# The MLP takes one chunk at a time, scores and maxima keep four PSUM banks, and 1.5 conversions of weights a slot in the first batch, not 1.2

## The chip, the cores and the metric

The kernel runs on one core of a Trainium2 chip. The metric is the device time of one execution in microseconds. It was 1240.38 us before the change, the median of three runs (1237.52 to 1241.49).

## What is computed

Attention with a decay, for 8 batches of 8 heads with 576 positions of size 64, and behind it an MLP with a squared ReLU on all 4608 tokens of width 512, with 2048 hidden units.

```python
scores = scale * np.matmul(q, k.transpose(0, 1, 3, 2))
cum = np.cumsum(np.log(np.clip(f, 0.0001, 1.0)), axis=-1)
decay = cum[:, :, :, None] - cum[:, :, None, :]
scores = np.where(causal, -1000000000.0, scores + decay)
scores = scores - np.max(scores, axis=-1, keepdims=True)
attn = np.exp(scores)
attn = attn / (np.sum(attn, axis=-1, keepdims=True) + 1e-09)
x = (attn @ v), heads side by side          # 4608 x 512
h = np.maximum(x @ w_in, 0.0)
out = h * h @ w_out
```

The two weight matrices come as 64-bit words, two 32-bit halves each.

## The kernel before

**Slots.** The program is written out by one loop over slots `n`. A slot is one unit of scores of one head; a head has six, a batch 48, and there are 384. In slot n the kernel writes the score matmul and the exponential of that unit (`score`; L363 and L365 on TensorE for heads below 14, L369 and L372 from head 14 on; L382 on ScalarE) and the product with the values of the unit two slots back (L430, or L407 to L409). From head 14 on the probabilities are split into two parts first (L397 on ScalarE, L398 on VectorE). The row maxima of a head are found ahead of its scores in six units of their own: a matmul (L324) into a PSUM bank and a reduction by VectorE out of it (L330), which frees the bank. Loads, the division (`finish`) and the preparation of heads (`prep`) stand at fixed slots in the tables at the end of the kernel. Each engine and SP's DMA queue execute in the order in which the loop writes; nothing overtakes on an engine.

**Weights.** 32 weight tiles of 512 KB (`w_in` and `w_out` in turn) have to be turned from 64-bit words into two parts of 32 bits. `weight_ops` is a generator of that work: two steps to begin with, then five a tile, four with an operation of VectorE (L189, L194, L199, L201) and the last with a cast by ScalarE (L206) and four subtractions by GpSimd (L210). Its loads (L169 on SP's queue) run up to four tiles ahead. `RATES` says how many steps a slot takes: its fifth number holds from slot 0 to slot 52, the sixth from slot 53 until the work is done.

**MLP.** The tokens are cut into 18 chunks of 256. A step `(c, fc)` of chunk c works on 128 of the hidden units: `mlp1` (twelve matmuls, L501, into bank 4; then L509 to L512 on ScalarE and VectorE) and, a step later, `mlp2` (six matmuls, L524, which add up in the two banks `o0` and `o1` over all 16 steps). A half step is one of the two. `mlp1` of step fc needs weight tile 2 fc, `mlp2` tile 2 fc + 1, and a step is begun when both are converted. Each time, `fill` writes as many half steps as a straight line from 0 to 64 over slots 53 to 104 asks for (two chunks in that time; once the weights are done, the line is drawn anew from where it stands); if `next_step` finds none that can be done, it leaves the rest to later slots. Before the change `next_step` takes chunk 0's next step if its weights are there, and otherwise chunk 1's, which walks over the same weights behind it.

**Banks.** PSUM has eight banks, given out in turn by use.

```python
    banks = {"av": [0, 6], "s": [1, 2, 3], "m": [4, 5, 7], "h": [4], "o0": [6], "o1": [7]}
```

Here `s` are the scores, `m` the maxima, `av` the products with the values, `h` the result of `mlp1`. From the first step of the MLP on `m` is empty, and maxima then take their bank from `s`. While chunks 0 and 1 are both under way, four banks hold sums, and `s` has two.

Of the kernel before, what the change touches and what calls it, by code (L numbers as in the profile page):

```python
# [36 lines left out]
def decay_attention_relu2_kernel(  # L37
# [26 lines left out]
    NF = w_in.shape[0]  # L64
# [18 lines left out]
    banks = {"av": [0, 6], "s": [1, 2, 3], "m": [4, 5, 7], "h": [4], "o0": [6], "o1": [7]}  # L83
# [75 lines left out]
    split_w = []  # L159
# [315 lines left out]
    mst = {}  # L475

    def split_x(c, finished):

        if c >= NCHUNK:
            return  # L480
        if ("x", c) not in mst:
            mst["x", c] = [wk.tile([P, NCC, T], F32R, name=x, bufs=1) for x in xnames[c % 2]], c * T
        (xh, xl), t0 = mst["x", c]
        while t0 < (c + 1) * T and t0 // S < finished:
            b = t0 // S
            t1 = min((b + 1) * S, (c + 1) * T)
            o, i = slice(t0 - c * T, t1 - c * T), slice(t0 - b * S, t1 - b * S)
            nc.vector.tensor_copy(out=xh[:, :, o], in_=xts[b][:, :, i])
            nc.vector.tensor_tensor(
                out=xl[:, :, o], in0=xts[b][:, :, i], in1=xh[:, :, o].bitcast(F32), op=ALU.subtract,  # L490
            )
            t0 = t1
        mst["x", c] = (xh, xl), t0

    def mlp1(c, fc):
        xh, xl = mst["x", c][0]
        ph = bank("h")
        w = split_w[2 * fc].rearrange("p s (c f) -> p s c f", f=P)
        for k, (s, x) in enumerate(((1, xh), (0, xh), (0, xl))):
            for cc in range(NCC):  # L500
                nc.tensor.matmul(  # L501
                    ph[:, :T], w[:, s, cc], x[:, cc, :],
                    start=(cc == 0 and k == 0), stop=(cc == NCC - 1 and k == 2),
                )
        r = wk.tile([P, T], F32, name="r", bufs=1)
        g = wk.tile([P, T], F32, name="g", bufs=1)
        gh = wk.tile([P, T], F32R, name="gh")
        gl = wk.tile([P, T], F32R, name="gl")
        nc.scalar.activation(out=r, in_=ph[:, :T], func=AF.Relu)  # L509
        nc.vector.tensor_tensor(out=g, in0=r, in1=r, op=ALU.mult)  # L510
        nc.scalar.activation(out=gh, in_=r, func=AF.Square)  # L511
        nc.vector.tensor_tensor(out=gl, in0=g, in1=gh.bitcast(F32), op=ALU.subtract)  # L512
        mst["g", c, fc] = (gh, gl)

    def mlp2(c, fc):
        if fc == 0:
            mst["o", c] = [bank(f"o{t}") for t in range(NTT)]
        gh, gl = mst.pop(("g", c, fc))
        w = split_w[2 * fc + 1]
        for t in range(NTT):  # L520
            po = mst["o", c][t]
            ts = slice(t * P, (t + 1) * P)
            for k, (g, s) in enumerate(((gh, 1), (gl, 0), (gh, 0))):
                nc.tensor.matmul(  # L524
                    po, g[:, ts], w[:, s],
                    start=(fc == 0 and k == 0), stop=(fc == NF - 1 and k == 2),
                )
            if fc == NF - 1:
                osb = wk.tile([P, DM], F32, name="osb")
                nc.scalar.copy(out=osb, in_=po)  # L530
                nc.sync.dma_start(out=out[c * T + t * P:c * T + (t + 1) * P, :], in_=osb)

    ahead = [0] * NCHUNK
# [3 lines left out]
    def next_step():  # L537

        for c in range(NCHUNK):
            fc = ahead[c]  # L540
            if fc < NF and len(split_w) >= 2 * (fc + 1):
                return c, fc
            if fc < NF and c > 0:
                return None

    def mlp_half(finished):
        if halves[0] % 2:
            if len(steps) > 1:
                mlp2(*steps[-2])
        else:  # L550
            step = next_step()
            if step is None:
                return False
            c, fc = step
            if fc == 0:
                if c == 0:
                    banks.update(s=[1, 2, 3, 5], m=[], av=[0])
                if c == 1:
                    banks.update(s=[1, 2], o0=[3], o1=[5])
                if c == 2:  # L560
                    banks.update(s=[1, 2, 3, 5], o0=[6], o1=[7])
                split_x(c, finished)
            if fc > 0 and ("x", c + 1) not in mst and (c != 1 or ahead[0] == NF):
                split_x(c + 1, finished)
            mlp1(c, fc)
            ahead[c] += 1
            steps.append(step)
        halves[0] += 1
        return True
# [2 lines left out]

    RATES = (1, 0, 2, 0, 1.2, 2.8)
    LAG = 2
    NA = H * NU

# [29 lines left out]
    def fill(n, part):  # L608

        b = sum(r <= n for r in ready)  # L610
        if b == 0:
            return
        r0 = ready[b - 1]
        r1 = ready[b] if b < B else r0 + H * NU
        limit, before = (2 * NF * (x * S // T) for x in (b, b - 1))
        goal = before + (limit - before) * (n - r0 + part) / (r1 - r0)
        if b == 1 and len(split_w) == NW:

            if not pace:
                pace.append((n + part, halves[0]))  # L620
            n0, h0 = pace[0]
            goal = h0 + (limit - h0) * (n + part - n0) / (r1 - n0)
        while halves[0] < min(goal, limit):
            split_last()
            if not mlp_half(b):
                break
# [4 lines left out]
    def cv(k):  # L631
        owed[0] += k
        convert(int(owed[0]))
        owed[0] -= int(owed[0])
# [53 lines left out]
    for n in range(-2 * NU, last_slot + 1):  # L688
# [17 lines left out]
        for do in events.get((n, 0), ()):  # L706
            do()
        wr = RATES[0 if n < -9 else 1 if n < -6 else 2 if n < -3 else 3 if n < 0 else 4 if n < ready[0] else 5]
        cv(wr / 2)
# [6 lines left out]
    while halves[0] < 2 * NCHUNK * NF:  # L716
        mlp_half(B)
# [42 lines left out]
```

## Time and profile before

| | |
|---|---|
| median of 3 runs | 1240.38 us |
| the profiled execution | 1240.59 us, of which the span is 1238.9 us |
| TensorE matmuls | 1186.2 us, 96% of the span |
| VectorE / ScalarE / GpSimd | 63% / 57% / 33% |
| first matmul of the MLP (L501) | at 110.95 us |
| chunk 0 done, chunk 1 done (first L530 of each) | at 223.3 and 278.6 us |

The span is what the profiler sees of the program, from its first instruction to its last. PE is TensorE, PEld its loading of weights, DVE VectorE, ACT ScalarE, POOL GpSimd, SP the engine whose queue issues most transfers (SPq). In a time line a row has the start, the duration, the engine, line and operation, what is written and read, and in brackets how long the engine stood idle before it and what ended that. In a table by stretches a row has the stretch, its length, the busy time and the number of instructions of each engine, then the granted clock of TensorE (PEclk, 1.00 is full), the busy share of the transfer engines and what they moved in GB/s. A group of instructions has its busy time, the mean duration of one in ns, and the idle time before them.

### The profile page before, as it was taken

What the parts mean: (1) busy time and instruction counts of PE and PEld (TensorE: products, weight loads), DVE (VectorE), ACT (ScalarE), POOL (GpSimd) and SP (SyncE); (2) the same over time, 40 slices, a digit from 0 to 9 for tenths busy, and PEclk for the clock granted to TensorE, in tenths of its full rate; (3) what the DMA queues carried; (4) which work ended last, traced back from release to release, by engine and by line L of the source; (5) the groups of instructions that cost most, each with busy time, mean ns of one, the idle gap of its engine ahead of it and who ended that gap; (6) DMA issues with size and microseconds to landing.
All of it is one profiled execution on the core that took longest, in us unless ns stands there. A gap on an engine that the chain in (4) does not pass through costs nothing.

```text
span 1238.9 us, 23313 instructions
## 1 busy us (share of the span) xinstructions
PE 1186.2 (96%) x7652; PEld 1051.3 (85%) x7652; DVE 778.6 (63%) x2044; ACT 701.6 (57%) x1720; POOL 411.1 (33%) x670
## 2 busy tenths in 40 slices
PE   5877998899999999999999999999999999999998
PEld 3655887778999899999999989998999899999997
DVE  6748876657676767666656666677676767533332
ACT  3644565456666666665565656666666666632332
POOL 3544446333333333333223233334333333200000
PEclk9998998899999999999999999999999999999999
DMA  7766540212121112121202121211121212000000
GB/s 201 173 161 169 147 122 16 52 32 58 41 58 36 49 35 54 41 58 27 58 17 53 31 58 36 54 36 49 42 58 41 58 41 57 13 27 1 18 18 18
DMA packets 114977, 71.62 MB, mean 58 GB/s; under 512 B 96908, under 2 KB 96908, under 8 KB 114856
## 3 DMA queue, kind: packets, MB, share of 16 engines
q1 hardware_dynamic: 113736, 66.00, 21.4%
q0 software_dynamic: 1120, 4.13, 1.5%
q8 instruction: 61, 1.00, 0.3%
q14 instruction: 60, 0.49, 0.1%
HBM read 59.90 MB, written 9.87 MB: 56 GB/s over the span
## 4 chain that ended last, share of the span: by engine, by line
PE 54%; ACT 1%; issue 1%; POOL 1%; DVE 0%; DMA 0%; SPq 0%; POOLq 0%; DVEq 0%
PE bank L501 22%; PE bank L524 21%; PE bank L407 2%; PE bank L372 2%; PE bank L409 2%; PE bank L324 2%; PE bank L408 2%; PE bank L369 2%; DMA den<-rdr 0%; ACT ph L397 0%; ACT den L446 0%; ACT r L509 0%; ACT p L382 0%; POOL p L384 0%; POOL v L310 0%
## 5 line engine op out<-in xcount | busy, mean ns | idle before, releaser
L524 PE MATMUL bank<-w,gh 128*128 128x512 f32 x1152 | 415.7, 401 | 0.0
L501 PE MATMUL bank<-xh,w 128*128 128x256 f32 x2304 | 332.2, 287 | 1.8 <-DVE tcol L330 1.7
L501 PEld LDWEIGHTS bank<-xh,w 128*128 128x128 f32 x2304 | 303.7, 191 | 9.9 <-DVE tcol L330 1.9
L398 DVE TENSOR_TENSOR pl<-p,ph 128x320 fp32r<-128x320 f32 (+4 forms) x300 | 186.5, 622 | 199.2 <-ACT ph L397 188.4
L524 PEld LDWEIGHTS bank<-w,gh 128*128 128x128 f32 x1152 | 218.6, 190 | 38.4
L524 PE MATMUL bank<-w,gl 128*128 128x512 f32 x576 | 227.5, 395 | 0.1
L509 ACT ACTIVATE r<-bank 128x256 f32<-128x256 f32 x288 | 110.5, 384 | 204.2 <-PE bank L501 192.1
L384 POOL TENSOR_SCALAR_AFFINE_SELECT p<-p 128x128 f32<-128x128 f32 (+1 forms) x250 | 82.1, 329 | 419.5 <-ACT p L382 275.2
L510 DVE TENSOR_TENSOR g<-r 128x256 f32<-128x256 f32 x288 | 126.0, 437 | 143.0 <-ACT r L509 142.4
L397 ACT CAST ph<-p 128x320 fp32r<-128x320 f32 (+4 forms) x300 | 124.4, 415 | 151.7 <-POOL p L384 150.0
L501 PE MATMUL bank<-xl,w 128*128 128x256 f32 x1152 | 185.8, 284 | 0.0
L501 PEld LDWEIGHTS bank<-xl,w 128*128 128x128 f32 x1152 | 159.7, 192 | 0.0
L330 DVE CUSTOM_DVE_ANT_0 bank<-bank,mz 128x256 f32<-128x256 f32 (+4 forms) x320 | 133.3, 433 | 40.9 <-PE bank L324 31.6
L382 ACT ACTIVATE p<-bank 128x320 f32<-128x320 f32 (+4 forms) x300 | 116.1, 387 | 65.1 <-PE bank L372 52.9
L512 DVE TENSOR_TENSOR gl<-g,gh 128x256 fp32r<-128x256 f32 x288 | 127.3, 442 | 35.8 <-ACT p L382 1.4
L324 PE MATMUL bank<-rk 66*128 66x320 f32 (+9 forms) x384 | 112.0, 323 | 32.2 <-DVE tcol L330 15.4
L511 ACT ACTIVATE gh<-r 128x256 fp32r<-128x256 f32 x288 | 120.5, 418 | 9.1
L524 PEld LDWEIGHTS bank<-w,gl 128*128 128x128 f32 x576 | 109.8, 191 | 14.3 <-DVE gl L512 0.9
L324 PEld LDWEIGHTS bank<-rk 66*128 66x128 f32 (+3 forms) x384 | 69.5, 188 | 44.8 <-DVE tcol L330 19.3
L210 POOL TENSOR_TENSOR w<-osb,w 128x128 fp32r<-128x128 f32 x128 | 72.3, 593 | 94.7 <-ACT w L206 64.6
L407 PE MATMUL bank<-pl,vh 128*65 128x320 f32 (+4 forms) x350 | 97.0, 277 | 2.3 <-ACT den L446 2.3
L408 PE MATMUL bank<-ph,v 128*64 128x320 f32 (+4 forms) x350 | 94.8, 271 | 0.0
(82 smaller groups left out, 1557.9 us busy)
## 6 DMA issues: line engine op xcount, KB each, us to landing
qkraw<-in_qk SPq DMA_DIRECT2D x50, 288.0 KB
v<-in_v SPq DMA_DIRECT2D x62, 160.0 KB
out<-osb SPq DMA_DIRECT2D x36, 256.0 KB
den<-rdr SPq DMA_DIRECT2D x62, 144.0 KB
w<-in_w_in SPq DMA_DIRECT2D x16, 512.0 KB
w<-in_w_out SPq DMA_DIRECT2D x16, 512.0 KB
rk<-in_qk POOLq DMA_DIRECT2D x14, 288.0 KB, 4.4
rl<-in_qk SPq DMA_DIRECT2D x14, 288.0 KB
```

What stands on the lines that cost most here:

```text
L324: nc.tensor.matmul(ps[:m, :n], st["r2"][:rows, q0:q0 + m], st["kl0"][:rows, k0:k0 + n], start=True, stop=True,)
L330: nc.vector.tensor_tensor_reduce(out=ps[:m, :n], in0=ps[:m, :n], in1=mz[:m, mo:mo + n], op0=ALU.add, op1=ALU.min, scale=-1.0, scalar=init, ...
L382: nc.scalar.activation(out=p[:kn, :n], in_=ps[:kn, :n], func=AF.Exp, scale=SCALE)
L397: nc.scalar.copy(out=ph[:, :n], in_=p[:, :n])
L398: nc.vector.tensor_tensor(out=pl[:, :n], in0=p[:, :n], in1=ph[:, :n].bitcast(F32), op=ALU.subtract,)
L407: nc.tensor.matmul(acc[:D + 1, o], vh, pl[:, i], start=first, stop=False)
L408: nc.tensor.matmul(acc[:D, o], vl, ph[:, i], start=False, stop=False)
L501: nc.tensor.matmul(ph[:, :T], w[:, s, cc], x[:, cc, :], start=(cc == 0 and k == 0), stop=(cc == NCC - 1 and k == 2),)
L510: nc.vector.tensor_tensor(out=g, in0=r, in1=r, op=ALU.mult)
L511: nc.scalar.activation(out=gh, in_=r, func=AF.Square)
L512: nc.vector.tensor_tensor(out=gl, in0=g, in1=gh.bitcast(F32), op=ALU.subtract)
L524: nc.tensor.matmul(po, g[:, ts], w[:, s], start=(fc == 0 and k == 0), stop=(fc == NF - 1 and k == 2),)
```

## The change

`next_step` takes the chunks strictly in order: if the weights of the next step of the earliest unfinished chunk are not there, nothing is done. So two chunks are never under way together; the sums are always in banks 6 and 7, and `s` keeps its four banks from slot 53 to the end. The condition that held back `split_x` of chunk 2 goes with it. The fifth rate is 1.5 in place of 1.2.

```diff
         for c in range(NCHUNK):
             fc = ahead[c]
-            if fc < NF and len(split_w) >= 2 * (fc + 1):
-                return c, fc
-            if fc < NF and c > 0:
-                return None
+            if fc < NF:
+                return (c, fc) if len(split_w) >= 2 * (fc + 1) else None
...
                     banks.update(s=[1, 2, 3, 5], m=[], av=[0])
-                if c == 1:
-                    banks.update(s=[1, 2], o0=[3], o1=[5])
-                if c == 2:
-                    banks.update(s=[1, 2, 3, 5], o0=[6], o1=[7])
                 split_x(c, finished)
-            if fc > 0 and ("x", c + 1) not in mst and (c != 1 or ahead[0] == NF):
+            if fc > 0 and ("x", c + 1) not in mst:
                 split_x(c + 1, finished)
...
-    RATES = (1, 0, 2, 0, 1.2, 2.8)
+    RATES = (1, 0, 2, 0, 1.5, 2.8)
```

What it does to the order is shown at three places. First TensorE at slots 91 and 92, where the first two units of head 16's maxima stand (L324), with a score (L369, L372) and a product with the values (L407 to L409) between them. Before:

```order
L324 MATMUL bank2_2582<-rk_0_68 128x256
L369 MATMUL bank1_2585<-rk_1_69 128x192
L372 MATMUL bank1_2585<-rl_2276 128x192
L407 MATMUL bank0_2591<-pl_2530,vh_1_73 65x320
L408 MATMUL bank0_2591<-ph_2529,v_2467 64x320
L409 MATMUL bank0_2591<-ph_2529,vh_1_73 65x320
L324 MATMUL bank2_2595<-rk_0_68 128x320
```

After, where the first unit, in bank2, stands in front of an `mlp2` of six matmuls, of which the last is shown:

```order
L524 MATMUL bank7_2213<-w13_918,gh_2479 128x512
L369 MATMUL bank3_2564<-rk_1_69 128x192
L372 MATMUL bank3_2564<-rl_2265 128x192
L407 MATMUL bank0_2570<-pl_2498,vh_1_73 65x320
L408 MATMUL bank0_2570<-ph_2497,v_2436 64x320
L409 MATMUL bank0_2570<-ph_2497,vh_1_73 65x320
L324 MATMUL bank5_2574<-rk_0_68 128x320
```

Before, both units use bank2; now the second has bank5, and the score between them bank3.

Second, TensorE from slot 78 to the first of head 14's maxima in slot 79. Before, from the end of the `mlp2` in slot 77 on:

```order
L524 MATMUL bank5_1915<-w3_357,gh_1951 128x512
L363 MATMUL bank2_2028<-rl_71 128x320
L430 MATMUL bank0_1903<-ph_1966,v_1677 128x320
L501 MATMUL bank4_2049<-xh0_1067,w26_1957 128x256 x8
L501 MATMUL bank4_2049<-xl0_1068,w26_1957 128x256 x4
L363 MATMUL bank1_2070<-rl_71 128x320
L365 LDWEIGHTS mz_66
L365 MATMUL bank1_2070<-p_67,mz_66 128x128
L430 MATMUL bank0_2075<-pl_2007,v_1677 128x256
L430 MATMUL bank0_2075<-ph_1966,v_1677 128x128
```

There an `mlp2` (six matmuls from weight tile 5) follows, and then the maximum. After, from the end of slot 77 on:

```order
L430 MATMUL bank0_1947<-pl_1967,v_1728 66x64
L363 MATMUL bank5_2040<-rl_71 128x320
L430 MATMUL bank0_1947<-ph_2006,v_1728 128x320
L363 MATMUL bank1_2063<-rl_71 128x320
L365 LDWEIGHTS mz_66
L365 MATMUL bank1_2063<-p_67,mz_66 128x128
L430 MATMUL bank0_2068<-pl_2026,v_1728 128x256
L430 MATMUL bank0_2068<-ph_2006,v_1728 128x128
L501 MATMUL bank4_2073<-xh0_1113,w30_2031 128x256 x8
L501 MATMUL bank4_2073<-xl0_1114,w30_2031 128x256 x4
L324 MATMUL bank2_2097<-rk_0_68 128x256
```

Slots 77 and 78 now have no half step of the MLP, and in slot 79 the `mlp1` of chunk 0's last step, which reads weight tile 30, stands in front of the maximum.

Third, SP's queue around the values of heads 5 and 6 in the first batch (`v`, and for head 6 `w31`, whose buffer it borrows; `cmp`, `rdr` and `den` belong to the division, `w11` and so on are weight tiles). Before:

```order
L460 DMA cmp_613<-den_490 64x1x9 x2
L169 DMA w11_618<-in_w_out 128x1024
L277 DMA v_627<-in_v 128x5x64
L465 DMA rdr_675<-cmp_613 128x9
L260 DMA rl_70<-in_qk 64x1152
L247 DMA rl_70<-cum_dr_74 2x576
L169 DMA w12_695<-in_w_in 128x1024
L352 DMA rl_70<-tcol_643 1x128x1 x4
L352 DMA rl_70<-tcol_643 1x64x1
L247 DMA rk_0_68<-cum_dr_74 2x576
L468 DMA den_490<-rdr_675 64x576 x2
L273 DMA w31_730<-in_v 128x5x64
```

After:

```order
L460 DMA cmp_638<-den_511 64x1x9 x2
L277 DMA v_653<-in_v 128x5x64
L169 DMA w13_669<-in_w_out 128x1024
L465 DMA rdr_701<-cmp_638 128x9
L260 DMA rl_70<-in_qk 64x1152
L247 DMA rl_70<-cum_dr_74 2x576
L352 DMA rl_70<-tcol_664 1x128x1 x4
L352 DMA rl_70<-tcol_664 1x64x1
L247 DMA rk_0_68<-cum_dr_74 2x576
L169 DMA w14_732<-in_w_in 128x1024
L468 DMA den_511<-rdr_701 64x576 x2
L273 DMA w31_760<-in_v 128x5x64
```

The weight moved from the front of head 5's values to behind them, and another now stands in front of head 6's; the values of heads 3 and 7 have a weight in front in both orders, those of head 2 only in the new one.

## The prediction

> **What bounds the kernel now.** I read the page's slices first, for where TensorE stands still, then busy time by stage, then what ended TensorE's waits in the stage that the diff names, and last the time lines around them.
>
> ```profile
> PE   5877998899999999999999999999999999999998
> PEclk9998998899999999999999999999999999999999
> ```
>
> Each digit is 31 us. From the ninth slice on TensorE is full at full clock; what can be won lies in the first eight, 250 us. To cut them I counted the exponentials of L382, one a slot (second table): slot 53, where the MLP starts, has its own at 108.9 us, slot 73 at 173.1, slot 84 (the first of head 14, with split scores) at 209.3, slot 104 at 274.0.
>
> ```profile
> core 0: us, PE busy (x) PEld busy (x) DVE busy (x) ACT busy (x) POOL busy (x), PEclk, DMA share, GB/s
> 21.60:108.90 87.30, 70.65 (x324) 47.91 (x323) 56.22 (x159) 45.90 (x111) 39.40 (x81) 0.93 0.74 177
> 108.90:173.10 64.20, 61.40 (x357) 51.34 (x356) 50.19 (x121) 35.90 (x83) 30.12 (x55) 0.96 0.60 163
> 173.10:209.30 36.20, 33.60 (x184) 27.68 (x183) 24.54 (x53) 18.95 (x46) 18.47 (x29) 0.91 0.09 22
> 209.30:274.00 64.70, 56.12 (x349) 48.88 (x348) 39.57 (x105) 37.30 (x92) 25.84 (x40) 0.95 0.19 43
> 299.30:407.40 108.10, 107.23 (x730) 97.67 (x730) 72.63 (x197) 71.06 (x177) 40.53 (x63) 1.00 0.20 47
> ...
> 209.30:274.00 64.70, 7.72 (x20) 0.95 0.19 43
> 299.30:407.40 108.10, 15.70 (x40) 1.00 0.20 47
> ```
>
> The stage 209.3 to 274.0 has the same kind of work as 299.3 to 407.4 (split heads, MLP in between), but two score banks, where the later stage has four. Its cost at the later stage's pace: two copies of finished sums in the pure MLP tail stand one chunk apart,
>
> ```profile
> 1145.82 1.16 ACT L530 COPY osb<-bank 128x512 f32<-128x512 f32 x2
> 1190.87 1.16 ACT L530 COPY osb<-bank 128x512 f32<-128x512 f32 x2
> ```
>
> 45.05 us for 32 half steps (an `mlp1` or an `mlp2`), 1.41 us each. The order of the program puts 53 half steps into the 40 slots of the later stage, so attention takes (108.1 - 53 x 1.41) / 40 = 0.83 us a slot. The stage with two banks has 20 slots and 25 half steps: 20 x 0.83 + 25 x 1.41 = 51.9 us, against 64.7 measured. So 12.8 us are lost there: 64.70 - 56.12 = 8.6 us idle, the rest at a lower clock. Who ended the idle time:
>
> ```profile
> PE bank L324 <- DVE tcol L330: 5.4, 3, 2.4
> PE bank L324 <- DVE rk L291: 1.5, 1, 1.5
> ...
> PE bank L324 <- ACT p L382: 0.3, 1, 0.3
> ```
>
> The longest of them, in TensorE's and VectorE's time line:
>
> ```profile
> 233.92 0.28 PE L324 MATMUL bank<-rk 66*128 66x256 f32 x1
> ...
> 234.78 1.20 DVE L398 TENSOR_TENSOR pl<-p,ph 128x320 fp32r<-128x320 f32 x1 [0.68 <-ACT ph L397]
> 235.91 0.41 DVE L510 TENSOR_TENSOR g<-r 128x256 f32<-128x256 f32 x1
> 236.43 0.42 DVE L512 TENSOR_TENSOR gl<-g,gh 128x256 fp32r<-128x256 f32 x1
> 236.77 0.43 DVE L330 CUSTOM_DVE_ANT_0 bank<-bank,mz 128x256 f32<-128x256 f32 x1
> ...
> 237.31 0.64 PE L324 MATMUL bank<-rk 66*128 66x320 f32 x1 [2.43 <-DVE tcol L330]
> ...
> 219.80:223.30 3.50, 3.50 (x15) 3.13 (x15) 3.04 (x12) 1.16 (x5) 1.48 (x2) 0.51 0.07 5
> 236.90:240.30 3.40, 2.99 (x7) 2.42 (x8) 1.19 (x5) 0.35 (x1) 0.25 (x2) 0.50 0.02 0
> ```
>
> A maximum's matmul ran at 233.92; VectorE first had a split and two MLP steps to do and came to the reduction at 236.77; the next maximum's matmul goes to the same bank and waited. The last two rows are the stretches behind the two longer such waits: the clock was half for 3.4 us each time, which costs 1.7 us of work.
>
> **The change, part by part.** *Banks and chunk order.* The two matmuls are the first two units of head 16's maxima. In the new order the first goes to bank2, the second to bank5, and a bank comes round again after three others. Then nothing stands between TensorE and the work behind. Gain: the waits of 5.4 and 0.3 us, and the two stretches of half clock behind them, 2 x 1.7: 9.1 us. What is late next: the wait on `DVE rk` and one on `cum_dr` stay, as they are waits for data. The bound above is the whole 12.8, the one below nothing, if TensorE ran into the next wait at once; the stage with four banks has 108.10 - 107.23 = 0.9 us idle in 40 slots, so I keep 9.1.
>
> The Trainium skill has a rule that speaks against part of this ("TensorE: Matmul & The Clock Gate", section "Why this matters for your kernels"): matmul throughput drops when TensorE is idle for more than about 3 us between bursts. By it these waits, 2.43 us at most, would not lower the clock, and the gain would be 5.7 us. The two rows with 0.51 and 0.50 do not agree with it.
>
> *Chunk 0 waits for its weights.* By the order, chunk 0's steps 0 to 14 find their weights converted by slot 76; before, chunk 1 filled in from slot 73. In slots 77 and 78 TensorE now has attention alone: at the maximum of slot 79 it has had two half steps less (2.8 us). That maximum was late already:
>
> ```profile
> 186.07 3.20 POOL L210 TENSOR_TENSOR w<-osb,w 128x128 fp32r<-128x128 f32 x4 [2.78 <-ACT w L206]
> 189.23 1.60 POOL L471 TENSOR_TENSOR xt<-xt,den 128x576 f32<-128x576 f32 x1
> 190.90 0.57 POOL L288 MEMSET rk<- 32x576 f32 x1
> 191.50 0.25 SPq L247 DMA_DIRECT2D rk<-cum_dr  x1
> ...
> 193.11 0.55 PE L324 MATMUL bank<-rk 66*128 66x256 f32 x1 [2.60 <-DMA rk<-cum_dr]
> ```
>
> A weight's subtraction, a product and a memset on POOL, then a transfer: 7.0 us from 186.07 to 193.11. Now the last step of chunk 0 stands in front of that matmul and needs weight 30, whose POOL part is the first link of the same chain. From the end of step 13's `gl`, VectorE has the rest of weight 29, one MLP pair and weight 30 to do; with the means quoted below 1.9 + 0.4 + 0.9 + 2.6 = 5.8 us (0.4 for two small operations on `cmp`), then the ACT cast, 0.6, and POOL's 2.2: 8.6. TensorE comes there after 1.41 and three slots of attention. Stage 108.9 to 173.1, 20 slots with 25 half steps at full load, gives (61.4 - 35.3) / 20 = 1.3 us a slot, so 5.3 us: it waits 3.3. Then product, memset, issue and transfer, 193.11 - 189.23 = 3.9 us, against the step's 1.41: another 2.5. Together 5.8 against 2.60 now: +3.2 us, and I take 2.9, since the small waits of VectorE for `r` go with the missing steps. Bounds: 0 (chain as long as before, the shift made good by a VectorE without conversions from slot 80 on), and 5.9 (both missing half steps lost, 2.8, and POOL one weight later, 3.1, the 3.20 of the row).
>
> *1.5 conversions a slot until slot 53.* 16 more steps there, three weights (17 done, not 14), and the same work less afterwards:
>
> ```profile
> L210 POOL TENSOR_TENSOR w<-osb,w 128x128 fp32r<-128x128 f32 x51 | 27.1, 558 | 43.3 <-ACT w L206 25.4 <-issue 17.9
> ...
> L201 DVE SCALAR_TENSOR_TENSOR osb<-w,osb 128x512 int32<-128x512 int32 x12 | 10.7, 891 | 0.2
> L199 DVE SCALAR_TENSOR_TENSOR osb<-w,osb 128x512 int32<-128x512 int32 x12 | 8.9, 745 | 0.2
> ...
> L206 ACT CAST w<-osb 128x512 fp32r<-128x512 f32 x13 | 8.0, 615 | 10.9 <-DVE osb L201 10.9
> ...
> L194 DVE TENSOR_SCALAR osb<-wmag 128x512 int32<-128x512 int32 x12 | 5.9, 495 | 0.5
> ...
> L189 DVE TENSOR_SCALAR wmag<-wmag 128x512 f32<-128x512 f32 x12 | 5.6, 466 | 0.0
> ```
>
> A weight takes 0.891 + 0.745 + 0.495 + 0.466 = 2.6 us of VectorE, two ACT operations (the other a wmag of about the same size) and 4 x 0.558 = 2.2 of POOL. Three weights are 7.8 us of VectorE, whose idle time in this stage is 87.30 - 56.22 = 31 us: hidden, except where its queue holds up a maximum. The batch's bound is rather SP's queue and the transfers:
>
> ```profile
> 62.25 0.58 SPq L169 DMA_DIRECT2D w<-in_w_out  x1
> 62.91 0.60 SPq L277 DMA_DIRECT2D v<-in_v  x1
> ...
> 49.09 0.78 PE L430 MATMUL bank<-ph,v 128*128 128x320 f32 x2 [1.47 <-DMA v<-in_v]
> 68.64 0.78 PE L430 MATMUL bank<-ph,v 128*128 128x320 f32 x2 [3.65 <-DMA v<-in_v]
> 89.49 0.78 PE L430 MATMUL bank<-ph,w 128*128 128x320 f32 x2 [3.93 <-DMA w<-in_v]
> 107.19 0.64 PE L324 MATMUL bank<-rk 128*128 128x320 f32 x1 [5.37 <-DVE tcol L330]
> ```
>
> TensorE waited three times for the values of an odd head (3, 5 and 7), each issued right behind a weight. In the new order heads 3 and 7 keep a weight in front, head 5 loses it, heads 2 and 6 get one. A weight in front costs its issue, 0.58, and its 512 KB: at the stage's 177 GB/s 3.0 us, an estimate, so at most 3.5. Head 5 should gain some 2.3 of its 3.65, heads 2 and 6 had no wait and may get one of 1 to 2 us each; three to four more issues of 0.58 are 2 us on a queue that TensorE follows here. The wait of 5.37 us at slot 51 (the reciprocal, then two conversion operations ahead of a maximum) has one such operation less behind the reciprocal: -0.6. -2.3 + 2 + 2 - 0.6 = 1.1; I take +1. Bounds: head 5's wait gone with a stretch of half clock, -3.65 - 1.7 = -5.4; and two new waits of 3.5 with their stretches, with SP's 2 us: 7 + 3.4 + 2 = +12.4.
>
> *The rest.* `split_x` for chunk 2 has its first 64 tokens at slot 80, not at 220 us: two small VectorE operations, nothing. Chunk 1's sums go to banks 6 and 7, free once chunk 0's are copied: an `mlp1` stands between, as at all later chunks, where TensorE stays full.
>
> *Sum:* 1240.6 (the profiled execution; span 1238.9, 1.7 around it; the median of the runs is 1240.4) - 9.1 + 2.9 + 1 = 1235.4; forecast 1235.
>
> **Rivals.** First, the two costs eat the gain: chunk 0's wait at its bound of 5.9 and the first batch +4: 1241.4, no change. For it: POOL's chain is already the latest there; against: VectorE has no conversions from slot 80 on.
>
> Second, slower: the first batch is bound by transfers (share 0.74, three of four long waits of TensorE behind a value load), and the added weights give heads 2 and 6 a full wait each with a half clock behind. At the +12.4 above: 1240.6 - 6.2 + 12.4 = 1246.8. It decides from 9.9 us of loss there (3.7 + 6.2). Against: only two heads get a weight in front and one loses it.
>
> Third, the clock is not won back: the waits go, the half clock stays, from whatever cause: 1240.6 - 5.7 + 2.9 + 1 = 1238.8, no change. The quoted stretches speak against it. That is also the result by the skill's rule on idle time.
>
> Fourth, the first batch gains, head 5's wait going with its half clock: 1240.6 - 6.2 - 5.4 = 1229.
>
> **How the numbers follow.** A measurement of this kernel tells about 0.3% (3.7 us) from no change. Chances: the forecast 0.55, first rival 0.17, slower 0.11, third 0.07, fourth 0.10. Faster: nearly all of the forecast's case and the fourth, 0.61; same: the first mostly, the third, a little of the forecast's, 0.25; slower 0.14. The range goes from the fourth case, 1229, past the first, to 1242; outside it lies the slower case and a little below.
>
> **What would show it.** Right: in the stage from head 14 to slot 104 no wait of L324 on `DVE tcol L330` over 0.5 us, granted clock 0.98 or more, and its length near 56 us. A wait of `mlp1` on POOL, or a longer one on `cum_dr`, in slot 79 shows the second step, its sum against 2.6 us its price. In the first batch the waits on `in_v` at heads 3, 5 and 7 (9.0 us now), and new ones at heads 2 and 6, show the third; MLP's first matmul, at 110.95 us now, should come within 2 us of that. Wrong: a first batch that ends over 5 us later or earlier, or waits on `DVE tcol` that stay with four banks.

## The result, and the profile after

The changed kernel takes 1230.04 us, the median of 7 runs (1226.71 to 1235.45); the kernel before, 1240.38. The ratio is 0.9921, with a 95% interval of 0.9897 to 0.9946: some 10 us faster, where 5 were forecast, inside the stated range and close to its lower end. The profiled execution is the slowest of the seven, 1235.45 us with a span of 1233.7. So its trace shows where time moved, but less of it than the median: it lies 5.1 us below the profiled execution before.

The slices of the changed kernel, to be laid beside those of before:

```profile
PE   5876998999999999999999999999999999999998
PEclk9897998999999999999999999999999999999999
```

In the eighth slice, 216 to 247 us, both digits are now 9, for 8 before; the seventh keeps its 8. Two early slices have become worse: the fourth has 6 for 7, and its clock 7 for 8; the clock of the second is 8 for 9.

The stage from head 14's first score to slot 104, busy time by engine as before:

```profile
215.00:271.00 56.00, 54.59 (x368) 49.50 (x367) 35.55 (x99) 36.24 (x91) 21.33 (x31) 1.00 0.17 37
```

and what ended TensorE's waits in it:

```profile
PE bank L324 <- DVE rk L291: 1.4, 1, 1.4
```

No wait on `DVE tcol` is left, the clock is 1.00, and the stage takes 56.0 us with 27 half steps of the MLP, not 64.7 with 25. Of the two waits for data that the prediction had kept, on `DVE rk` and on `cum_dr`, the first stayed and the second is gone. TensorE's waits in the two stages in front of it, first from 21.6 to 118.0, then from there to 215:

```profile
PE bank L324 <- DVE tcol L330: 4.5, 3, 4.0
PE bank L430 <- DMA v<-in_v: 4.4, 3, 3.1
PE bank L430 <- DMA w<-in_v: 2.8, 1, 2.8
...
PE bank L430 <- ACT den L446: 1.5, 1, 1.5
PE bank L324 <- DMA rk<-cum_dr: 1.3, 1, 1.3
PE bank L501 <- POOL w L210: 0.5, 1, 0.5
```

The MLP's first matmul comes at 118.0 us, not 110.95: in this execution the first batch has become 7 us longer. What the later runs need is read off the time lines of all profiles in the same way; here it is in one table, in us. "First batch" ends with the MLP's first matmul (L501), "to head 14" with its first score (L369), "to slot 104" with the first matmul of head 18's maxima, at the end of slot 103, "to slot 112" with that slot's score. Half steps of the MLP differ only up to head 14's first score, and are given with it; one takes 1.41 us. From slot 112 to the end all take 939 to 941. The profiled executions are not all typical ones: those of the changed kernel lie 5.4 and 3.1 us above the medians of their runs, those of `rate_only` and `late_rate` 2.3 and 3.5 below, the second of before 4.5 below. So the table shows places better than sizes.

| kernel | first batch | to head 14 (half steps) | to slot 104 | to slot 112 | profiled execution |
|---|---|---|---|---|---|
| before, two profiles | 110.9, 111.8 | 96.9, 95.5 (38) | 65.6, 64.9 | 24.9, 23.4 | 1240.6, 1237.0 |
| changed, two profiles | 118.0, 116.0 | 96.2, 95.0 (36) | 56.2, 55.7 | 23.3, 23.3 | 1235.5, 1231.8 |
| `rate_only` | 113.5 | 94.4 (38) | 58.7 | 25.0 | 1232.5 |
| `order_only` | 112.9 | 86.3 (29) | 70.5 | 23.4 | 1234.8 |
| `two_banks` | 113.6 | 96.3 (36) | 59.1 | 27.3 | 1238.6 |
| `late_rate` | 109.1 | 105.8 (38) | 60.8 | 23.4 | 1241.4 |
| `order_late` | 111.1 | 107.0 (36) | 56.9 | 23.6 | 1240.3 |
| `rate_18` | 120.6 | 93.0 (39) | 53.4 | 24.7 | 1234.8 |

### The profile page after: what moved, and what is told of

Same layout as the page of the kernel before. It is cut to its first block, busy times and chain, and to the rows that moved or that the text cites. A ratio compares the mean times of both kernels' runs of the same rounds, so it can differ in the third digit from the quotient of the medians.

```text
span 1233.7 us, 23332 instructions
## 1 busy us (share of the span) xinstructions
PE 1185.7 (96%) x7652; PEld 1050.8 (85%) x7652; DVE 772.9 (63%) x2044; ACT 701.1 (57%) x1720; POOL 410.9 (33%) x670
## 4 chain that ended last, share of the span: by engine, by line
PE 64%; ACT 2%; issue 1%; POOL 1%; DVE 0%; DMA 0%; SPq 0%; POOLq 0%; DVEq 0%
PE bank L501 25%; PE bank L524 24%; PE bank L407 3%; PE bank L372 2%; PE bank L409 2%; PE bank L324 2%; PE bank L408 2%; PE bank L369 2%; ACT den L446 0%; ACT r L509 0%; ACT p L382 0%; DMA den<-rdr 0%; ACT ph L397 0%; POOL v L310 0%; ACT gh L511 0%
## 5 line engine op out<-in xcount | busy, mean ns | idle before, releaser
L501 PE MATMUL bank<-xh,w 128*128 128x256 f32 x2304 | 331.8, 287 | 2.8 <-DVE tcol L330 2.2
L501 PEld LDWEIGHTS bank<-xh,w 128*128 128x128 f32 x2304 | 302.9, 190 | 11.3 <-DVE tcol L330 2.4
L398 DVE TENSOR_TENSOR pl<-p,ph 128x320 fp32r<-128x320 f32 (+4 forms) x300 | 182.2, 607 | 201.7 <-ACT ph L397 192.9
L510 DVE TENSOR_TENSOR g<-r 128x256 f32<-128x256 f32 x288 | 129.1, 448 | 145.1 <-ACT r L509 144.4
L501 PE MATMUL bank<-xl,w 128*128 128x256 f32 x1152 | 185.1, 283 | 0.0
L501 PEld LDWEIGHTS bank<-xl,w 128*128 128x128 f32 x1152 | 159.0, 191 | 0.0
L512 DVE TENSOR_TENSOR gl<-g,gh 128x256 fp32r<-128x256 f32 x288 | 126.0, 438 | 35.1 <-PE bank L524 0.5
L324 PE MATMUL bank<-rk 66*128 66x320 f32 (+9 forms) x384 | 111.8, 322 | 22.9 <-DMA rk<-qkraw 9.9
L511 ACT ACTIVATE gh<-r 128x256 fp32r<-128x256 f32 x288 | 120.6, 419 | 9.1
L210 POOL TENSOR_TENSOR w<-osb,w 128x128 fp32r<-128x128 f32 x128 | 72.7, 596 | 79.4 <-ACT w L206 42.3
L407 PE MATMUL bank<-pl,vh 128*65 128x320 f32 (+4 forms) x350 | 96.8, 277 | 2.4 <-ACT den L446 2.4
L324 PEld LDWEIGHTS bank<-rk 66*128 66x128 f32 (+3 forms) x384 | 69.8, 189 | 33.4 <-issue 13.1
```

Of the source, the lines that this page charges most:

```text
L324: nc.tensor.matmul(ps[:m, :n], st["r2"][:rows, q0:q0 + m], st["kl0"][:rows, k0:k0 + n], start=True, stop=True,)
L398: nc.vector.tensor_tensor(out=pl[:, :n], in0=p[:, :n], in1=ph[:, :n].bitcast(F32), op=ALU.subtract,)
L407: nc.tensor.matmul(acc[:D + 1, o], vh, pl[:, i], start=first, stop=False)
L501: nc.tensor.matmul(ph[:, :T], w[:, s, cc], x[:, cc, :], start=(cc == 0 and k == 0), stop=(cc == NCC - 1 and k == 2),)
```

## The experiments

**Both kernels again.** No edit.

> The changed kernel once more, to see how far its executions lie apart and where. Its first profiled execution took 1235.45 us, the median of its runs 1230.0. Theory A: the banks are worth some 10 us in every execution, and the first batch differs from execution to execution by the stretches of half clock that its waits set off (7 us longer than before in that first profile, 2 us longer in a typical one). Then a second profile has the stage of head 14 to slot 104 within 1 us of the first (its PE idle about 1.5 us), and differs, if at all, ahead of the MLP's first matmul, which was at 118.0 us. Rival B: the executions differ in the later stages, by transfers or clock there; then the MLP's first matmul comes at 118 us again while the whole differs.

> The kernel before once more, for a second profile of it. Theory D: the stage from head 14's first score to slot 104 is over 62 us long again (65.6 in the first profile), with waits of L324 on DVE tcol, and the MLP's first matmul is at 110 to 113 us. If the first profile was an exception there (stretches of half clock by chance), the stage is under 60 us.

The changed kernel gave 1228.67 us (6 runs, 1227.06 to 1232.09; ratio 0.9905, 0.9875 to 0.9935), its second profile 1231.8; the kernel before 1241.56 (8 runs, 1237.02 to 1248.11). The second profile of the changed kernel has the stage of head 14 within 0.5 us of the first, as theory A had it; of the 3.7 us between the two executions 2.0 lie in the first batch and 1.2 in the stage behind it. The second profile of before has a stage of 64.9 us and the waits on `DVE tcol` again (second row below, of that profile, from 207.3 to 272.2):

```profile
PE bank L324 <- DVE tcol L330: 5.7, 4, 2.4
...
207.30:272.20 64.90, 56.09 (x350) 48.47 (x349) 41.10 (x106) 38.20 (x95) 26.36 (x40) 0.97 0.18 43
```

So the long stage of the kernel before was no accident. Its half clock was partly one: 0.95 in one profile, 0.97 in the other.

**Two banks in the changed kernel.** Order and rate stay, but the scores and maxima have banks 1 and 2 alone while chunk 1 is under way.

```diff
                     banks.update(s=[1, 2, 3, 5], m=[], av=[0])
+                if c == 1:
+                    banks.update(s=[1, 2])
+                if c == 2:
+                    banks.update(s=[1, 2, 3, 5])
```

> The changed kernel, but while chunk 1 is under way (slots 80 to 104) scores and maxima take turns in banks 1 and 2 alone; banks 3 and 5 lie idle. Order and rate are those of the change. Theory A: the waits of L324 on DVE tcol come back, 5 to 6 us with their stretches of half clock, and the time is 1237 to 1242 us. Rival C, and any theory by which the chunk order or the earlier end of the conversions gives the gain: 1228 to 1233, as the changed kernel.

1239.01 us (12 runs, ratio to before 0.9981, 0.9962 to 1.0), against 1228.67 on the same chip with four banks: 10.3 us for the banks alone, as theory A had it. The waits stand in its profile again, in the stage from 210 to 269.5 and in the one behind, to 297:

```profile
PE bank L324 <- DVE tcol L330: 2.6, 3, 1.3
...
PE bank L324 <- DVE tcol L330: 2.2, 1, 2.2
...
269.00:297.00 28.00, 25.43 (x163) 22.82 (x163) 19.41 (x52) 14.87 (x39) 10.19 (x15) 0.94 0.14 37
```

4.8 us of waits and, behind the 2.2, a clock of 0.94 over 28 us, 1.7 us. In the profiles the two stages are together 7.4 us longer than with four banks (59.1 + 27.3 against 55.7 + 23.3). But the waits stand at other units than in the kernel before: the longest at head 15's fourth, head 17's second and head 18's second maximum (1.3, 1.1 and 2.2 us). At head 16's second, in slot 92, where the kernel before waits 2.43 us, it is 0.15 us with the same two banks: in the changed order an `mlp2` stands between the two units.

**The rate alone.** The kernel before, with the one number changed.

```diff
-    RATES = (1, 0, 2, 0, 1.2, 2.8)
+    RATES = (1, 0, 2, 0, 1.5, 2.8)
```

> The kernel before with 1.5 conversions a slot in the first batch; the two chunks at once and the two score banks stay. Theory A (the gain is the banks', the rate only costs in the first batch): 1242 to 1247 us, with the waits of L324 on DVE tcol in the stage from head 14 to slot 104 as before (about 5 us). Rival C (the gain is the rate's: conversions are done earlier and leave VectorE and POOL free for the stage behind): 1236 or less.

1234.78 us (12 runs, ratio 0.9946, 0.9925 to 0.9966): a miss of theory A. The rate gains some 6 us by itself, with two chunks at once and two banks. By the table it pays 2 us in the first batch and gets back 6 to 7 in the stage from head 14 to slot 104. That stage, 208 to 267 us:

```profile
PE bank L324 <- DVE tcol L330: 3.2, 3, 2.0
...
208.00:267.00 59.00, 53.57 (x354) 47.38 (x352) 36.93 (x99) 35.94 (x90) 20.11 (x32) 1.00 0.17 38
```

There are still waits for banks, but 3.2 us of them, not 5.4 or 5.7, and VectorE and POOL have less to do in the stage (36.9 and 20.1 us, against 39.6 and 25.8). In the kernel before the last subtraction of a weight (L210) ends at 215.0 us, 7 us after head 14's first score; here it ends at 195.2, 13 us ahead of it.

**The order and the banks alone.** The changed kernel with 1.2.

```diff
-    RATES = (1, 0, 2, 0, 1.5, 2.8)
+    RATES = (1, 0, 2, 0, 1.2, 2.8)
```

> The changed kernel with 1.2 conversions a slot. Chunk 0 is out of converted weights from slot 73 on and done only near slot 85, so that TensorE has some 8 half steps (11 us) too few in slots 73 to 85 and they come later, where TensorE is full. Theory A: the banks still gain 10 us, the missing half steps cost most of their 11, the first batch is as before: 1236 to 1242 us. Rival C: with the rate undone nothing is gained and the starvation is paid: 1248 or more. A third view, that the starvation is free because POOL and VectorE are the limit there anyway: 1230.

1234.28 us (9 runs, ratio 0.9938, 0.9915 to 0.9962), 2 us better than theory A's lower end. The nine half steps that are missing at slot 84 (29 for 38) do come later, and that stage is 5 us longer than before in spite of its four banks (70.5 us to slot 104, for 65.6 and 64.9); the stage ahead of it becomes some 10 us shorter (86.3 for 96.9 and 95.5). Against the kernel before on the same chip, 1241.39, the rate alone gives -6.6 us and the order with its banks -7.1, -13.7 by addition; the whole gave -10.3 and -12.7 in its two measurements.

**The same rate's gain, without its price?** The kernel before with an unchanged first batch, but more steps behind it, so that the conversions end at the same slot as with 1.5; and the same in the changed kernel.

```diff
-    RATES = (1, 0, 2, 0, 1.2, 2.8)
+    RATES = (1, 0, 2, 0, 1.2, 3.4)
```

> The kernel before (two chunks at once, two score banks), its first batch untouched at 1.2 conversions a slot, but 3.4 a slot from slot 53 on, so that the conversions end near slot 79 and not 84. It is to tell why the rate of 1.5 alone gave 1234.8 us. Theory D: the gain is that the conversions are over before head 14's first split score; its price is paid in the first batch (2 to 4 us in the profiles). Then this gains the same without that price: 1230 to 1235. Rival E: the gain is in slots 53 to 79 or comes with a first batch in which more is done; then 3.4 a slot only loads VectorE more in a stretch where it is busy 50.2 of 64.2 us: 1239 or more.

> The changed kernel with rates of 1.2 and 3.4 in place of 1.5 and 2.8: chunks in order, four banks, conversions over near slot 79 as in the change, the first batch as before the change. Theory D: as the changed kernel (1228.7 to 1230.0) less the first batch's 2 to 4 us: 1226 to 1229. Rival F: VectorE, with 3.4 steps of about 0.65 us a slot beside the MLP, becomes the bound in slots 53 to 79, where a slot takes 3.1 us: 1231 or more, with waits of L501 on POOL w L210 there.

1244.95 us (12 runs, ratio 1.0034, 1.0016 to 1.0051) and 1240.29 (12 runs, ratio 0.9994, 0.9977 to 1.001): theory D's numbers were wrong both times, E and F were right. The profiles say how. `late_rate`, from the MLP's first matmul to head 14 and from there to slot 104, and what TensorE waited for in the first of these:

```profile
109.10:214.90 105.80, 96.13 (x529) 78.20 (x530) 75.35 (x173) 55.21 (x127) 52.06 (x90) 0.94 0.38 105
214.90:275.70 60.80, 55.26 (x351) 48.27 (x349) 37.63 (x99) 35.96 (x90) 19.91 (x30) 0.97 0.18 45
...
PE bank L324 <- DMA rk<-cum_dr: 4.4, 1, 4.4
PE bank L430 <- ACT den L446: 2.6, 2, 1.8
```

The stage behind the conversions does gain (60.8 us, for 65 before): that much of theory D stands. But the stretch in which 3.4 steps a slot run beside the MLP is 9 to 10 us longer (105.8 for 96.9 and 95.5). So the same work costs less in the first batch than beside the MLP: all the conversions are 160 steps whichever way, and `late_rate` and `rate_only` differ only in where 16 of them lie, with 10 us between their medians (on two chips, against 1240.3 and 1241.4 for the kernel before). `order_late` and the changed kernel differ in the same way, by 11.6 us (1240.29 and 1228.67).

**More of it.** The changed kernel with 1.8, by which chunk 0 never runs out of weights.

```diff
-    RATES = (1, 0, 2, 0, 1.5, 2.8)
+    RATES = (1, 0, 2, 0, 1.8, 2.8)
```

> The changed kernel with 1.8 conversions a slot in the first batch: chunk 0 never runs out of weights (by the order no slot from 53 on lacks a half step), conversions end near slot 74. Theory I (a conversion costs less beside the first batch than beside the MLP, whichever chunk order, and the lack of half steps in slots 77 and 78 costs a little): the first batch is 4 us longer once more (the MLP's first matmul at 117 to 121 us), the stretch from there to head 14's first maximum 2 to 4 us shorter than its share, and the time 1228 to 1232. Rival J (the second step of the prediction is right at 2.9 us, and the first batch hides most of its conversions): 1225 to 1227.

1234.94 us (9 runs, ratio 0.9952, 0.9934 to 0.997): outside both. The first batch is longer by as much as theory I had it (120.6 us), and the stretch to head 14 has three half steps more in 2 to 3 us less, but that is not enough. In the stretch from 120.6 to 213.6, TensorE's waits are

```profile
PE bank L501 <- DVE tcol L330: 2.5, 1, 2.5
PE bank L430 <- ACT den L446: 1.3, 2, 1.0
```

with none on `cum_dr` or on a weight, which suggests that the lack of half steps in slots 77 and 78 does cost something at 1.5. Its price by itself is not separated from that of the other conversions.

**The first batch's loads.** The changed kernel with the values of heads 2 to 7 two slots earlier; then, besides, the zeros of a head's last unit by VectorE.

```diff
-        at((h - 1) * NU + VLOAD, 1, load_v, h)
+        at((h - 1) * NU + (VLOAD - 2 if 1 < h < H else VLOAD), 1, load_v, h)
...
-            nc.gpsimd.memset(p[kn:, :n], 0.0)
+            (nc.vector if h < H else nc.gpsimd).memset(p[kn:, :n], 0.0)
```

> The changed kernel with the values of heads 2 to 7 loaded two slots earlier (on SP's queue ahead of the division's loads and of the weight that stood in front). The waits on in_v in the first batch were 7.2 us in the first profile after. Theory G (a late load is what holds TensorE up there, and the half clock follows): the waits on in_v fall under 1.5 us and the time is 1222 to 1226. Rival H (the first batch is bound by SP's issues or by the transfers as a whole, and the wait only moves to the next load or to VectorE): 1227 to 1231.

> The values two slots earlier, and besides the zeros in the lower half of a head's last unit (64 by 64 and so on) written by VectorE instead of GpSimd in the first batch. With the values early, TensorE's waits on in_v were 0.4 us and those on that memset 4.5 us, behind the weights' subtractions on GpSimd. Theory G2 (each late thing in the first batch can be taken out in turn): 1224 to 1227 us. Rival H (the first batch is bound by SP's issues and the transfers as a whole, the wait moves on): 1227 to 1231, as both changed kernels.

1228.77 us (6 runs, ratio 0.9911, 0.989 to 0.9931) and 1228.15 (6 runs, ratio 0.9902, 0.9875 to 0.993), against 1228.67 and 1230.04 for the changed kernel: no gain that can be told. What TensorE waited for in the first batch, first with the values early, then with both:

```profile
PE bank L430 <- POOL pl L381: 4.5, 4, 2.1
PE bank L430 <- ACT den L446: 4.0, 4, 1.6
PE bank L324 <- DVE tcol L330: 3.3, 3, 2.5
PE bank L363 <- DMA rl<-tcol: 3.1, 2, 2.1
...
PE bank L430 <- DMA v<-in_v: 0.4, 1, 0.4
...
PE bank L430 <- issue: 5.3, 4, 2.7
PE bank L363 <- DMA rl<-tcol: 3.8, 3, 1.9
PE bank L324 <- DVE tcol L330: 2.7, 6, 1.0
...
PE bank L430 <- DMA v<-in_v: 1.9, 1, 1.9
```

The waits on `in_v`, 7.2 us in the first profile of the changed kernel, are down to 0.4 us with the values early, and their time has moved to a memset, the division's copies, the maxima and their transfers. With the memset moved as well, the memset's wait is gone, but TensorE stands still for 5.3 us ahead of products with the values (L430) without a releaser that the profile shows (`issue`), and 1.9 us are again put on the values. That is rival H by the medians. In the two profiles the first batch is shorter (112.6 and 109.2 us, where the changed kernel's two have 118.0 and 116.0), but the medians of the whole do not show it.

## Why the prediction was right, and where it was not

**Banks: right in the sum, and in place for the changed kernel.** -9.1 us were put on the waits for a bank and the half clock behind them; `two_banks` says 10.3, of which its profile shows 6.5 as waits and half clock. The waits were where they were said to be, and none is left with four banks. But the wait that the prediction took as its example, 2.43 us in slot 92, does not need four banks to go: with two it is 0.15 us in `two_banks`, and `rate_only` shows none. The number of banks and the place of the half steps both decide it.

**Half clock behind a wait: seen, but not a rule.** The prediction put 1.7 us on each longer wait. The runs show that it differs from execution to execution. In `rate_only` the same wait as in the first profile before, for the same bank, in the same slot, left the clock alone (the row from 213 to 222 us has it in the middle):

```profile
215.35 0.42 PE L324 MATMUL bank<-rk 66*128 66x320 f32 x1 [1.97 <-DVE tcol L330]
...
213.00:222.00 9.00, 6.71 (x40) 5.48 (x39) 6.11 (x19) 3.12 (x10) 2.97 (x5) 1.00 0.04 3
```

while in the kernel before the wait of 1.98 us was followed by 3.5 us at 0.51. In the second profile of the kernel before, the wait at this place, 2.06 us, left it alone too. This may be one cause for the scatter of single executions (1226.7 to 1235.5): the seven executions of the changed kernel have a mean clock between 0.985 (the slowest) and 0.993. By the rule of the Trainium skill that the prediction cites ("TensorE: Matmul & The Clock Gate", section "Why this matters for your kernels") neither wait would have lowered the clock; one of the two did.

**Chunk 0 waits for its weights: mechanism right, size not settled.** +2.9 us were put on it, with 5.8 of waits against 2.6. In the two profiles the waits of slots 77 to 79 are 1.5 + 0.5 + 1.3 = 3.3 and 1.5 + 0.5 + 2.2 = 4.2 us, so +0.7 and +1.6. `mlp1` did wait on POOL and then the maximum on `cum_dr`, as said, but 0.5 and not 3.3 us on the first: part of the time went to a copy of the division (`den L446`), which TensorE met first, and POOL had no backlog. The medians say more than the waits: `two_banks` and `rate_only` have the same rate and two score banks (from slots 80 and 76 to slot 104), differ in the order of the chunks, and lie 4.2 us apart (1239.01 and 1234.78). That holds the price of the order, but also where the half steps fall.

**The first batch: the size was off.** +1 us was taken, from bounds of -5.4 and +12.4, and the MLP's first matmul was to come within 2 us of 110.95. A first batch that ends over 5 us later was named as a sign of being wrong, and both profiles of the changed kernel show it (118.0 and 116.0). Five profiles with 1.2 have the MLP's first matmul at 109.1 to 112.9 us (mean 111.2), four with 1.5 at 113.5 to 118.0 (mean 115.3): +4; without the changed kernel's two, which lie above their medians, +2.4. The reading of the queue held for some heads: in both profiles after, head 5's wait for its values (3.65 us before) is gone, and head 6 has a new one, in the first

```profile
PE bank L430 <- DMA w<-in_v: 2.8, 1, 2.8
```

and in the second 0.9 us. That second profile has 3.5 us at head 8, which no step had foreseen. And the sum is more than the value loads, as `v_early` shows: with them early other waits of the batch took their place.

**The step that failed** is the clause "and the same work less afterwards". It gave the 16 conversion steps that leave slots 53 to 84 no price, though the same paragraph named VectorE's idle time in the first batch (31 us) and its load beside the MLP stands in the first table (50.2 of 64.2 us). Four kernels measured on one chip show the size without any profile: the kernel before 1241.39, `rate_only` 1234.78, `order_only` 1234.28, the changed kernel 1228.67. Order and banks give -7.1 us at the old rate and -6.1 at the new; the forecast had -9.1 + 2.9 = -6.2. The rate gives -6.6 in the old order and -5.6 in the new; the forecast had +1. So order and banks came as forecast in sum, and the rate's term had the wrong sign. With +2 to +4 us in the first batch, what the rate gains behind it is some 8 to 11 us; in the profiles, from the MLP's first matmul to slot 112, it is 185.6 (mean of before) less 178.1 us, 7.5, and with the order changed 180.2 less 174.9 (mean of two), 5.3.

That the time still fell into the stated range is partly luck. Its lower end, 1229, stood for a first batch that gains; the first batch lost, and the time came near that end by a gain that had been left out. The second measurement, 1228.67, lies just below it.

Not all of that gain is a price of conversions. In the stage from head 14 on, `rate_only` loses the 2.43 us of slot 92, seven slots behind the last conversion of the kernel before. There the half steps have moved. TensorE and VectorE around head 16's first two maxima, first in `rate_only`, then in `late_rate`, which has the `mlp1` in front of the first maximum as the kernel before has:

```profile
230.57 0.39 PE L324 MATMUL bank<-rk 66*128 66x256 f32 x1 [0.53 <-DVE rk L291]
230.79 1.12 PE L501 MATMUL bank<-xh,w 128*128 128x256 f32 x8
230.99 0.43 DVE L330 CUSTOM_DVE_ANT_0 bank<-bank,mz 128x256 f32<-128x256 f32 x1
...
232.84 0.42 DVE L510 TENSOR_TENSOR g<-r 128x256 f32<-128x256 f32 x1
232.86 0.32 PE L324 MATMUL bank<-rk 66*128 66x320 f32 x1
...
236.68 0.64 PE L501 MATMUL bank<-xl,w 128*128 128x256 f32 x4
237.15 0.28 PE L324 MATMUL bank<-rk 66*128 66x256 f32 x1
...
238.54 0.41 DVE L510 TENSOR_TENSOR g<-r 128x256 f32<-128x256 f32 x1
239.06 0.42 DVE L512 TENSOR_TENSOR gl<-g,gh 128x256 fp32r<-128x256 f32 x1
239.40 0.43 DVE L330 CUSTOM_DVE_ANT_0 bank<-bank,mz 128x256 f32<-128x256 f32 x1
...
239.94 0.41 PE L324 MATMUL bank<-rk 66*128 66x320 f32 x1 [1.87 <-DVE tcol L330]
```

With the `mlp1` behind the maximum, its operations on VectorE (L510, L512) come after the reduction, and the bank is free in time; with it in front they come before, and TensorE waits 1.87 us, with all conversions over by 198.1 us. So this part of the gain is the place of a half step. What stays open is how the rest divides between the conversions themselves and the half steps that move with them, and why a conversion costs more beside the MLP: VectorE's load there is the likely reason, but no run separates it.

## What to carry to other kernels

Where two matmuls of a chain of reductions take turns in two PSUM banks with other matmuls between them, the second waits for the queue that stands ahead of the first one's reduction; look at the release of the bank, and at which side job stands in front of the first matmul, not at the load of the engine. A side job that is spread over stages has a different price in each: price what leaves a stage as carefully as what enters one. Here the idle time of the engine that it uses showed the direction (VectorE idle for 31 of 87 us in the first batch, for 14 of 64 beside the MLP), but not the size. And where single executions scatter by nearly as much as the effect, as here by 9 us, one profile shows the place of a gain but not its size.

## What the runs showed of the hardware

A VectorE operation that reads two operands took longer while GpSimd ran one of two operands. In the kernel before, the split of a unit (L398) that delayed the bank in slot 91, and the one before it, ran while GpSimd had a product or a subtraction; a third, with GpSimd at rest, took 0.48 us:

```profile
232.33 1.43 POOL L471 TENSOR_TENSOR xt<-xt,den 128x576 f32<-128x576 f32 x1 [3.00 <-DMA den<-rdr]
232.83 1.28 DVE L398 TENSOR_TENSOR pl<-p,ph 128x320 fp32r<-128x320 f32 x1 [0.98 <-ACT ph L397]
234.23 1.41 POOL L298 TENSOR_TENSOR rl<-qkraw,rk 64x576 fp32r<-64x576 f32 x1
271.21 0.48 DVE L398 TENSOR_TENSOR pl<-p,ph 128x320 fp32r<-128x320 f32 x1
```

The second of the slow ones, at 234.78 with 1.20 us, stands in the prediction's time line. Over the whole trace, 52 operations of this size without such company took 0.49 us (median, at most 0.58), 48 with it 0.86 (at most 1.28). On GpSimd the weights' subtractions (L210) took 0.46 us (median of 76) with no such VectorE operation beside them, and 0.64 (median of 48) where one overlapped more than 30% of their time; for the division's product (L471) no difference shows (1.46 and 1.44). The prediction took such durations from the rows as they stood; part of the price of conversions beside the MLP may be this, since each has four subtractions on GpSimd, but no run here separates it.
